# Up products of a gated block in eleven instead of twelve block products, with the stages beside them re-placed

## The chip, the cores and the metric

The kernel runs on one core of a Trainium2 chip. The metric is device time in microseconds (us), the median of several executions. The span in a profile is a little shorter than that time (628.2 us against 629.93 in the profiled run of the changed kernel). The first four executions of the kernel before span 0.25%, those of the changed kernel 0.7%. All executions that are compared here were of the fast state.

## The reference, cut to what matters

```python
# attention, for each of 4 batches and 8 heads, 768 tokens, head dimension 48
f = 1 / (1 + exp(-f_logit))
for t in range(S):
    state = f[t, :, None] * state + outer(k[t], v[t])
    y[t] = q[t] @ state
# x: the outputs as (3072 tokens, 384 channels)
a = x @ w_a            # 384 -> 1536
b = x @ w_b            # 384 -> 1536
out = (a * b) @ w_out  # 1536 -> 384
```

All of it is float32. The two products with `w_a` and `w_b` are called the up products here, the one with `w_out` the down product.

## The kernel before

Tokens come in eight blocks of 384, two per batch. A block needs two attention units, so there are 16 units. Each unit has stages on several engines: ScalarE's sigmoids, VectorE's scans, and small products on TensorE. A queue puts these stages between the large products.

The up product of one of the 12 output tiles takes three channel tiles for each of the two factors, 384 tokens at a time. ScalarE copies b out of PSUM, and VectorE multiplies it with a:

```python
def up(blk, ft):
    x, ps = xT[blk], {}
    for nm, w in (("b", w_b), ("a", w_a)):
        ps[nm] = ps_f.tile([128, 512], ...)[:, 0:BLK]
        for kt in range(NKT):                       # 3 channel tiles
            nc.tensor.matmul(ps[nm], lhsT=w[:, kt, ft * 128:ft * 128 + 128], rhs=x[:, kt],
                             start=kt == 0, stop=kt == NKT - 1)
    factors.append((blk, ft, ps))

def product():
    blk, ft, ps = factors.pop(0)
    b_sb = sb2.tile([128, BLK], ...)
    nc.scalar.copy(b_sb, ps["b"])
    # ...
    nc.vector.tensor_tensor(products[blk, part][:, :, i], a, b, ALU.mult)
```

The down product already works on pairs of token groups in seven instead of eight block products of 192 columns, with VectorE forming the sums (`s1` to `s4`) and the results. The kernel keeps TensorE's results in tiles of one memory, PSUM (a tile of 128x512 is called a bank here), and its operands in another, SBUF. Four PSUM banks serve up and down products together.

A unit's stages (the code is cut), and when they come (in steps; one output tile is a step, a down product is 3.5):

```python
def slot(u):                       # six calls, each up to the next yield
    within(u - 1); scores(u)       # TensorE; VectorE's mask
    yield
    next(nxt); yield               # unit u + 1: sigmoids (ScalarE)
    turn(u); across(u - 1); yield  # TensorE; ScalarE's copies
    next(nxt); yield               # scans of f (VectorE)
    gains(u); yield                # TensorE; VectorE's states
    next(nxt); next(nxt); yield    # scans of 1/f, products of q and k (VectorE)
# ...
at, when = m * a_batch + (-13.4, -0.8, 4.9, 13)[i], (0, 1, 2.2, 2.8, 3.4, 3.9)
```

## Time and profile before

| | before |
|---|---|
| time, median of 4 runs | 649.7 us |
| TensorE busy | 95% of 647.9 us |
| weight loads busy | 68% |
| VectorE, ScalarE busy | 45%, 29% |
| one instruction of 384 columns, undisturbed (46.64 us of the chain / 144) | 323.9 ns |
| one instruction of 192 columns, undisturbed (27.31 us / 168) | 162.6 ns |

A float32 product is two matmul instructions (1152 of L451 for 576 products). TensorE has no gap after 75 us (busy for 566.9 of the 566.9 us to the last product's end). This is the timeline of two halves of a tile in the last block (start, length, engine, line, operation, shapes; in brackets the idle time before and what ended it):

```profile
569.63 1.80 PEld L451 LDWEIGHTS f<-xT,w_a 128*128 128x128 f32 x6
569.95 2.10 PE L451 MATMUL f<-xT,w_a 128*128 128x384 f32 x6
570.20 0.48 ACT L466 COPY b_sb<-f 128x384 f32<-128x384 f32 x1 [5.89 <-PE f L451]
571.56 1.80 PEld L451 LDWEIGHTS f<-xT,w_b 128*128 128x128 f32 x6
571.88 2.10 PE L451 MATMUL f<-xT,w_b 128*128 128x384 f32 x6
572.15 0.56 DVE L471 TENSOR_TENSOR ab<-f,b_sb 128x384 f32<-128x384 f32 x1 [3.78 <-PE f L451]
573.50 1.80 PEld L451 LDWEIGHTS f<-xT,w_a 128*128 128x128 f32 x6
573.82 2.10 PE L451 MATMUL f<-xT,w_a 128*128 128x384 f32 x6
```

From start to start, the 12 instructions between 569.95 and 573.82 take 322.5 ns each. That is 1.4 ns less than the table has, because a piece's length also takes in its two ends (46.64 us less 144 x 322.5 ns leaves 0.2 us).

The lines show how loose this stretch is. ScalarE and VectorE each wait microseconds for TensorE, and TensorE writes a bank again only a whole tile later.

### The profile page before, as it was taken

Reading aid. Unit: us, or ns where it says so; the run is one execution under the profiler, and the core shown is the slowest. Engines: PE = TensorE matmul, PEld = TensorE weight load, DVE = VectorE, ACT = ScalarE, POOL = GpSimd, SP = SyncE. Lnnn points to the kernel's source line nnn. Section 1 sums busy time; section 2 is a strip of 40 time slices with the busy share of each in tenths; the row PEclk is TensorE's granted clock in tenths of the full one; section 3 lists DMA queues with packets and bytes.
Section 4 is the critical chain, followed back from the end, with each engine's and each line's share of the span. In section 5 each row is a group of like instructions: output and inputs, shape, how many; then the busy total and the mean of one; then the engine's idle time right before and its main releaser. Section 6 shows DMA issues by size and latency. Waiting matters only on the chain.

```text
span 647.9 us, 12250 instructions
## 1 busy us (share of the span) xinstructions
PE 614.6 (95%) x5202; PEld 442.0 (68%) x5202; DVE 289.7 (45%) x572; ACT 187.0 (29%) x328; POOL 65.6 (10%) x58
## 2 busy tenths in 40 slices
PE   0859899999999999999999999999999999999996
PEld 0626555559997566856698666966689655965696
DVE  6778345587774427161642345352444021311241
ACT  6577599632221322211201222122200212011100
POOL 6243154320010000000000000000000000000000
PEclk9969999999999999999999999999999999999999
DMA  9885874000332303130400124040001000000000
GB/s 223 232 266 157 193 260 147 1 2 2 97 92 72 92 1 92 38 80 1 93 24 26 47 46 92 14 105 1 19 1 37 14 19 19 1 26 0 1 24 30
DMA packets 30336, 43.56 MB, mean 67 GB/s; under 512 B 3776, under 2 KB 24896, under 8 KB 30272
## 3 DMA queue, kind: packets, MB, share of 16 engines
q1 hardware_dynamic: 29984, 42.38, 24.0%
q8 instruction: 43, 0.70, 0.4%
q10 hardware_dynamic: 288, 0.30, 0.2%
q14 instruction: 21, 0.17, 0.1%
HBM read 33.23 MB, written 4.72 MB: 59 GB/s over the span
## 4 chain that ended last, share of the span: by engine, by line
PE 92%; DMA 4%; ACT 1%; SPq 1%; DVE 0%; ACTq 0%; issue 0%; DVEq 0%
PE f L451 58%; PE f L508 26%; DMA xT<-y 2%; PE ps_y L409 2%; PE ps_y L388 2%; PE ps_x L354 2%; PE ps_x L308 2%; PE ps_x L335 1%; DMA q_in<-in_q_dram 1%; DMA raw<-in_moe_w_a_dram 1%; SPq L145 0%; PE f L335 0%; ACTq L436 0%; DVE y L422 0%; ACT bit L204 0%
## 5 line engine op out<-in xcount | busy, mean ns | idle before, releaser
L451 PE MATMUL f<-xT,w_b 128*128 128x384 f32 x576 | 206.9, 495 | 7.3 <-DVE w_b L211 5.6
L451 PE MATMUL f<-xT,w_a 128*128 128x384 f32 x576 | 203.4, 490 | 0.0
L451 PEld LDWEIGHTS f<-xT,w_a 128*128 128x128 f32 x576 | 110.2, 192 | 77.6 <-issue 2.3
L451 PEld LDWEIGHTS f<-xT,w_b 128*128 128x128 f32 x576 | 107.0, 191 | 78.6 <-DVE w_b L211 6.7
L471 DVE TENSOR_TENSOR ab<-f,b_sb 128x384 f32<-128x384 f32 x96 | 53.0, 555 | 199.1 <-PE f L451 147.9
L466 ACT COPY b_sb<-f 128x384 f32<-128x384 f32 x96 | 45.6, 476 | 228.9 <-PE f L451 219.6
L508 PE MATMUL f<-raw,h 128*128 128x192 f32 x432 | 73.7, 328 | 0.0
L508 PEld LDWEIGHTS f<-raw,h 128*128 128x128 f32 x432 | 70.2, 190 | 0.5
L261 POOL TENSOR_SCALAR inv<-inv 128x768 f32<-128x768 f32 x16 | 18.0, 1123 | 333.1 <-ACT inv L257 333.0
L508 PE MATMUL f<-w_out,ab 128*128 128x192 f32 x288 | 51.0, 327 | 0.0
L508 PEld LDWEIGHTS f<-w_out,ab 128*128 128x128 f32 x288 | 47.5, 190 | 1.8
L200 POOL TENSOR_SCALAR h<-h 128x768 f32<-128x768 f32 (+1 forms) x20 | 40.7, 2035 | 51.4 <-ACT h L197 49.7
L503 DVE TENSOR_TENSOR o<-f,u 128x192 f32<-128x192 f32 x36 | 12.9, 357 | 57.3 <-PE f L508 57.1
L308 PE MATMUL ps_x<-q_in,k_in 48*64 48x64 f32 x672 | 13.6, 226 | 15.6 <-DVE start L271 15.6
L276 DVE TENSOR_TENSOR_SCAN inv<-inv,start,zero 128x128 f32<-128x128 f32 x64 | 27.5, 471 | 0.0
L324 DVE TENSOR_TENSOR at<-ps_x,causal 128x768 f32<-128x768 f32 x14 | 13.4, 955 | 29.0 <-PE ps_x L308 29.0
L508 PE MATMUL f<-raw,ab 128*128 128x192 f32 x144 | 25.7, 328 | 0.0
L508 PE MATMUL f<-w_out,h 128*128 128x192 f32 x144 | 25.4, 326 | 0.0
L266 DVE TENSOR_TENSOR_SCAN f_in<-f_in,zero 128x384 f32<-128x384 f32 x28 | 25.2, 940 | 0.0
L370 DVE TENSOR_TENSOR st<-st,ps_x 128x96 f32<-128x96 f32 x80 | 20.2, 253 | 10.5 <-PE ps_x L354 8.0
L339 ACT COPY kT<-ps_x 128x768 f32<-128x768 f32 x12 | 9.6, 800 | 51.3 <-PE ps_x L335 51.3
L422 ACT COPY y<-ps_y 48x384 f32<-48x384 f32 (+1 forms) x43 | 20.5, 476 | 13.0 <-PE ps_y L409 8.4
(91 smaller groups left out, 456.6 us busy)
## 6 DMA issues: line engine op xcount, KB each, us to landing
q_in<-in_q_dram SPq DMA_DIRECT2D x32, 144.0 KB, 4.4
k_in<-in_k_dram SPq DMA_DIRECT2D x32, 144.0 KB, 3.7
v_in<-in_v_dram SPq DMA_DIRECT2D x16, 288.0 KB, 4.9
raw<-in_moe_w_out_dram SPq DMA_DIRECT2D x6, 768.0 KB, 4.2
out_dram<-o SPq DMA_DIRECT2D x24, 192.0 KB, 1.9
f_in<-in_f_logit_dram SPq DMA_DIRECT2D x28, 144.0 KB, 3.1
xT<-y SPq DMA_DIRECT2D x46, 72.0 KB, 2.2
raw<-in_moe_w_b_dram SPq DMA_DIRECT2D x4, 768.0 KB, 7.3
```

The lines of the kernel that those rows point to most:

```text
L200: nc.gpsimd.tensor_scalar(h, h, HI_MAX, None, ALU.min)
L261: nc.gpsimd.tensor_scalar(inv, inv, EXP_K, 1.0, ALU.mult, ALU.add)
L266: nc.vector.tensor_tensor_scan(F[:, c], F[:, c], none, math.exp(MIDDLE), ALU.mult, ALU.add)
L276: nc.vector.tensor_tensor_scan(inv[:, w], inv[:, w], none[:, 0:C], first, ALU.mult, ALU.add)
L308: nc.tensor.matmul(ps[h][SUB * p:SUB * p + SUB, o:o + SUB], lhsT=kf[r, tokens(n, c, p)], rhs=qf[r, tokens(n, c, p)], start=True, stop=True,)
L324: nc.vector.tensor_tensor(to, x, tri.broadcast_to((128, *lead, 2 * NC, SUB)), ALU.mult)
L370: nc.vector.tensor_tensor(st[:, j], before, new, ALU.add)
L422: copy(y[r:r + rows, :, p], ps[p][e:e + rows, 0:BLK].rearrange("r (o m) -> r o m", m=SUB))
L451: nc.tensor.matmul(ps[nm], lhsT=w[:, kt, ft * 128:ft * 128 + 128], rhs=x[:, kt], start=kt == 0, stop=kt == NKT - 1,)
L466: nc.scalar.copy(b_sb, ps["b"])
L471: nc.vector.tensor_tensor(products[blk, part][:, :, i], a, b, ALU.mult)
L508: nc.tensor.matmul(to, lhsT=x[:, i], rhs=w[:, i], start=first and i == 0, stop=i == HFT - 1, skip_group_check=True)
```

## The change

From block 2 on, two output tiles, two channel tiles and two token halves make a 2x2 by 2x2 product, done in seven block products by sums; the third channel tile is added in four. That is eleven products of 192 columns per factor in place of twelve. The additions go to VectorE, the intermediate results through ScalarE into SBUF. The units' stages are cut and placed anew. Storage is shared to make room: one tile `groups` for the products and the pair's scratch, one for `spare` combinations, and a single `inv` scratch for the later units.

```diff
+    def up_pair(blk, j):
+        # ... blocks a11..a22 of the weights, b11..b22 of the tokens, a1, a2, b1, b2 the third channel tile
+        order = (0, 1, 2, 3) if next(turns) else (2, 3, 0, 1)
+        x0, x1, m0, m1 = (ps_f[i][:, 0:2 * HT].rearrange("p (g t) -> p g t", g=2) for i in order)
+        # times(): for both factors g, one product = two instructions of 192 columns each
+        times(x0, a11, b11, True)
+        nc.scalar.copy(p1, x0)
+        times(x1, a12, b21, True)
+        times(m1, s1, t1, True)
+        nc.scalar.copy(p5, m1)
+        times(x0, s2, t2)
+        nc.scalar.copy(u2, x0)
+        times(m0, a22, t4, True)
+        times(m0, a2, b1)
+        times(x0, s3, t3)
+        nc.scalar.copy(u3, x0)
+        add(1, 0, m0, u3)
+        yield
+        times(m1, s4, b22)
+        times(m1, a1, b2)
+        add(0, 1, m1, u2)
+        times(x1, a1, b1)
+        add(0, 0, x1, p1)
+        times(x0, a2, b2)
+        add(1, 1, x0, p5)
+        # ... two multiplications a * b
+        yield
# ...
     def slot(u):
+        next(nxt, None)              # sigmoids
+        yield
         if u > 2 * NQ: within(u - 1)
         if u < NU: scores(u)
-        yield
         next(nxt, None)              # scans of f
         yield
         # turn(u), across(u - 1)
         yield
-        next(nxt, None)
-        yield
         # gains(u)
         yield
         next(nxt, None)              # scans of 1/f
+        yield
         next(nxt, None)              # products of q and k
         yield
# ... when the stages come, in steps of half a pair, by the unit's place in its batch
+                (2.6, 3.6, 4.6, 5.6, 7.6, 9.6),
+                (10.6, 12.3, 13.3, 14.3, 17.1, 19.1),
+                (20.1, 21.1, 22.1, 23.1, 25.1, 27.8),
+                (28.8, 29.8, 30.3, 31.3, 33.3, 36.1),
```

(The remarks in the code are mine.) The first `yield` of a pair is its middle, the second its end.

More of the change, by code (lines that the diff above doesn't have):

```diff
@@ L1 @@
+import itertools
 import math
@@ L65 @@
     ident = fixed([128, 128], "ident")
-    w_a = fixed([128, NKT, DFF], "w_a")
-    w_b = fixed([128, NKT, DFF], "w_b")
+    w_ba = fixed([128, 2, NKT, DFF], "w_ba")
     w_out = fixed([128, NFT, DM], "w_out")
     bad = fixed([1, 1], "bad", I32)
-    weights = (w_a, w_b, w_out)
+    weights = (w_ba, w_out)
     with ExitStack() as pools:
@@ L81, in by_quotients @@
     B, H, D, S = q.shape
-    w_a, w_b, w_out = weights
-    NKT, NFT, DM = w_a.shape[1], w_out.shape[1], out.shape[1]
+    w_ba, w_out = weights
+    w_b, w_a = (w_ba[:, i] for i in range(2))
+    NKT, NFT, DM = w_ba.shape[2], w_out.shape[1], out.shape[1]
     NH = S // BLK
@@ L98, in by_quotients @@
     sb3 = ctx.enter_context(tc.tile_pool(name="sb3", bufs=3))
-    ab_pool = ctx.enter_context(tc.tile_pool(name="ab", bufs=4))
     raw_pool = ctx.enter_context(tc.tile_pool(name="raw", bufs=4))
     ps_a = ctx.enter_context(tc.tile_pool(name="ps_a", bufs=1, space=bass.MemoryType.PSUM))
-    ps_f = ctx.enter_context(tc.tile_pool(name="ps_f", bufs=4, space=bass.MemoryType.PSUM))
     def fixed(shape, name):
@@ L119, in by_quotients @@
     whole = fixed([128, 1], "whole")
-    sign = fixedp.tile([128, PIECE], BF16, tag="sign", name="sign")
-    bits = [fixedp.tile([128, PIECE], U32, tag=f"bit{i}", name=f"bit{i}") for i in range(3)]
+    groups = fixed([128, 2 * NTG, NFT * 128], "groups")
+    spare = fixed([128, 3 * HFT * (DM // 2)], "spare")
+    bits = [spare[:, PIECE * i:PIECE * i + PIECE].bitcast(U32) for i in range(3)]
+    sign = spare[:, 3 * PIECE:3 * PIECE + PIECE // 2].bitcast(BF16)
+    invs = [fixed([128, 2 * BLK], "inv"), spare[:, 3 * PIECE + PIECE // 2:3 * PIECE + PIECE // 2 + 2 * BLK]]
     tails = fixed([128, NU], "tails")
@@ L178, in load_weights @@
                 if len(raws) in EARLY:
-                    raw = ab_pool.tile([128, NTG * HFT * 128 // 2], mybir.dt.uint64, tag="ab", name="ab")
+                    raw = groups[:, EARLY.index(len(raws))].bitcast(mybir.dt.uint64)
                 else:
@@ L241, in by_quotients @@
     live = {}
-    firsts = ab_pool.tile([128, NQ, 2, BLK], FP32, tag="ab", name="ab")
+    firsts = groups[:, len(EARLY)].rearrange("p (u n s) -> p u n s", u=NQ, n=2)
     products_of_f = {u: firsts[:, u] if u in FIRST else sets[u % NSET]["f"] for u in range(NU)}
@@ L253, in front @@
         F = halves(products_of_f[u])
-        inv = sb2.tile([128, 2 * BLK], FP32, tag="inv", name="inv")
+        inv = invs[u % 2 if u < 2 * NQ else 0]
         if u in FIRST:
@@ L285, in by_quotients @@
     y_banks = [ps_y[:, p] for p in range(2)]
+    ps_f = [ps_a.tile([128, 512], FP32, tag=f"ps_f{i}", name=f"ps_f{i}") for i in range(4)]
+    idle = list(range(4))
+    turns = itertools.cycle((0, 1))
     def tokens(n, c, p):
@@ L296, in pair, with give_back @@
     def pair(spare=False):
-        return [ps_f.tile([128, 512], FP32, tag="f", name="f") if spare else ps_x[:, i] for i in range(2)]
+        return [ps_f[idle.pop(0)] if spare else ps_x[:, i] for i in range(2)]
+    def give_back(ps):
+        idle.extend(i for x in ps for i, bank in enumerate(ps_f) if bank is x)
     def scores(u, spare=False):
@@ L325, in scores @@
         live[u]["at"] = at
+        give_back(ps)
     def turn(u, spare=False):
@@ L340, in turn @@
         live[u]["kT"] = kT
+        give_back(ps)
     def gains(u):
@@ L422, in across @@
             copy(y[r:r + rows, :, p], ps[p][e:e + rows, 0:BLK].rearrange("r (o m) -> r o m", m=SUB))
+        give_back(ps)
         y = y.rearrange("r (n c) p m -> r n (c p m)", n=2)
@@ L440, in across, with products @@
             load_unit(u + NSET)
-    products = {}
+    def products(blk):
+        first = (NTG, 0)[blk] if blk < 2 else blk % 2
+        return groups[:, first:first + NTG].rearrange("p g (k t) -> p g k t", k=NFT)
     factors = []
@@ L448, in up @@
         for nm, w in (("b", w_b), ("a", w_a)):
-            ps[nm] = ps_f.tile([128, 512], FP32, tag="f", name="f")[:, 0:BLK]
+            ps[nm] = ps_f[idle.pop(0)]
             for kt in range(NKT):
                 nc.tensor.matmul(
-                    ps[nm],
+                    ps[nm][:, 0:BLK],
                     lhsT=w[:, kt, ft * 128:ft * 128 + 128],
@@ L465, in product @@
         b_sb = sb2.tile([128, BLK], FP32, tag="b_sb", name="b_sb")
-        nc.scalar.copy(b_sb, ps["b"])
-        part, i = divmod(ft, HFT)
-        if i == 0:
-            products[blk, part] = ab_pool.tile([128, NTG, HFT, 128], FP32, tag="ab", name="ab")
-        a, b = (x.rearrange("p (g t) -> p g t", g=NTG) for x in (ps["a"], b_sb))
-        nc.vector.tensor_tensor(products[blk, part][:, :, i], a, b, ALU.mult)
+        nc.scalar.copy(b_sb, ps["b"][:, 0:BLK])
+        a, b = (x.rearrange("p (g t) -> p g t", g=NTG) for x in (ps["a"][:, 0:BLK], b_sb))
@@ new lines, in product, with by_pairs, combine_w_ba @@
+        nc.vector.tensor_tensor(products(blk)[:, :, ft], a, b, ALU.mult)
+        give_back(ps.values())
+    HT = BLK // 2
+    sums_of_w, sums_of_x = [], {}
+    def by_pairs(k):
+        w = w_ba[:, :, k].rearrange("p g (j two c) -> p g two j c", two=2, c=128)
+        return w[:, :, 0], w[:, :, 1]
+    def combine_w_ba():
+        (a11, a21), (a12, a22) = by_pairs(0), by_pairs(1)
+        for _ in range(4):
+            raw = raw_pool.tile([128, PIECE], mybir.dt.uint64, tag="raw", name="raw")
+            sums_of_w.append(raw.bitcast(FP32).rearrange("p (g j c) -> p g j c", g=2, c=128))
+        s1, s2, s3, s4 = sums_of_w
+        for to, x, y, op in (
+            (s3, a11, a21, ALU.subtract),
+            (s1, a21, a22, ALU.add),
+            (s2, s1, a11, ALU.subtract),
+            (s4, a12, s2, ALU.subtract),
+        ):
+            for g in range(2):
+                nc.vector.tensor_tensor(to[:, g], x[:, g], y[:, g], op)
+            yield
@@ new lines, in blocks_of_x, with combine_x @@
+    def blocks_of_x(blk, k):
+        return (xT[blk][:, k, HT * i:HT * i + HT] for i in range(2))
+    def combine_x(blk):
+        (b11, b12), (b21, b22) = blocks_of_x(blk, 0), blocks_of_x(blk, 1)
+        tiles = (sb2.tile([128, BLK], FP32, tag="b_sb", name="b_sb") for _ in range(2))
+        t1, t2, t3, t4 = sums_of_x[blk] = [t[:, HT * i:HT * i + HT] for t in tiles for i in range(2)]
+        for to, x, y in ((t1, b12, b11), (t2, b22, t1), (t3, b22, b12), (t4, b21, t2)):
+            nc.vector.tensor_tensor(to, x, y, ALU.subtract)
@@ new lines, in up_pair, with times, add @@
+    def up_pair(blk, j):
+        (a11, a21), (a12, a22), (a1, a2) = (by_pairs(k) for k in range(NKT))
+        (b11, b12), (b21, b22), (b1, b2) = (blocks_of_x(blk, k) for k in range(NKT))
+        s1, s2, s3, s4 = sums_of_w
+        t1, t2, t3, t4 = sums_of_x[blk]
+        order = (0, 1, 2, 3) if next(turns) else (2, 3, 0, 1)
+        x0, x1, m0, m1 = (ps_f[i][:, 0:2 * HT].rearrange("p (g t) -> p g t", g=2) for i in order)
+        p1, p5, u2, u3 = groups[:, 2 * NTG - 1].rearrange("p (i g t) -> i p g t", i=4, g=2)
+        c = groups[:, 2 * NTG - 2].rearrange("p (g k i t) -> p g k i t", g=2, k=2, i=2)
+        def times(to, w, x, start=False):
+            for g in range(2):
+                nc.tensor.matmul(
+                    to[:, g], lhsT=w[:, g, j], rhs=x, start=start and g == 0, stop=True, skip_group_check=True
+                )
+        def add(k, i, x, y):
+            nc.vector.tensor_tensor(c[:, :, k, i], x, y, ALU.add)
+        times(x0, a11, b11, True)
[18 more added lines that the diff above has]
+        add(1, 1, x0, p5)
+        b, a = (c[:, g].rearrange("p k i t -> p k (i t)").rearrange("p k (g t) -> p g k t", g=NTG) for g in range(2))
+        to = products(blk)
+        for k in range(2):
+            nc.vector.tensor_tensor(to[:, :, 2 * j + k], a[:, :, k], b[:, :, k], ALU.mult)
+        yield
@@ L482, in combine_w_out @@
         )
-        for _ in range(4):
-            raw = raw_pool.tile([128, PIECE], mybir.dt.uint64, tag="raw", name="raw")
-            combos.append(raw.bitcast(FP32)[:, 0:HFT * HM].rearrange("p (k m) -> p k m", k=HFT))
-        t1, t2, t3, t4 = combos
-        nc.vector.tensor_tensor(t3, b22, b12, ALU.subtract)
+        combos.extend(spare.rearrange("p (i k m) -> i p k m", i=3, k=HFT))
+        t1, t2, t4 = combos
+        combos.insert(2, b12)
         nc.vector.tensor_tensor(t1, b12, b11, ALU.subtract)
@@ L490, in combine_w_out @@
         nc.vector.tensor_tensor(t4, b21, t2, ALU.subtract)
+        nc.vector.tensor_tensor(b12, b12, b22, ALU.subtract)
     def down(pair):
-        (blk0, g0), (blk1, g1) = pair
         b11, b21, b22 = (w_out[:, HFT * i:HFT * i + HFT, HM * j:HM * j + HM] for i, j in ((0, 0), (1, 0), (1, 1)))
         t1, t2, t3, t4 = combos
-        a11, a21 = products[blk0, 0][:, g0], products[blk1, 0][:, g1]
+        (blk0, g0), (blk1, g1) = pair
+        a11, a12 = (products(blk0)[:, g0, HFT * i:HFT * i + HFT] for i in range(2))
+        a21, a22 = (products(blk1)[:, g1, HFT * i:HFT * i + HFT] for i in range(2))
         def block():
@@ L510, in times @@
                 )
-        s3 = add(block(), a11, a21, ALU.subtract)
+        s3 = add(block(), a21, a11, ALU.subtract)
         yield
-        x, m = (ps_f.tile([128, 512], FP32, tag="f", name="f") for _ in range(2))
+        x, m = ps_f[0:2] if next(turns) else ps_f[2:4]
         x0, x1, m0, m1 = (t[:, HM * i:HM * i + HM] for t in (x, m) for i in range(2))
@@ L519, in down @@
         product()
-        a12, a22 = products[blk0, 1][:, g0], products[blk1, 1][:, g1]
         s1 = add(block(), a21, a22)
@@ L571, in slot @@
         next(nxt, None)
+        yield
         next(nxt, None)
@@ L710, in by_quotients @@
             if b:
-                rest += [(up, 2 * b, ft) for ft in range(NFT)] + [(down, b, tuple(even[0:2]))]
-                rest += [(up, 2 * b + 1, ft) for ft in range(NFT)]
-            else:
-                rest += [(down, b, tuple(even[0:2]))]
-            rest += [(down, b, (even[2], odd[0])), (down, b, tuple(odd[1:]))]
+                rest += [(up_pair, 2 * b, j) for j in range(NFT // 2)] + [(down, b, tuple(even[1:]))]
+                rest += [(up_pair, 2 * b + 1, j) for j in range(NFT // 2)]
+            else:
+                rest += [(down, b, tuple(even[1:]))]
+            rest += [(down, b, (even[0], odd[0])), (down, b, tuple(odd[1:]))]
         slots = {s: slot(s) for s in range(2 * NQ, NU + 1)}
@@ L719, in by_quotients @@
         queue = [(2 * NFT - 4 + d, fronts[2 * NQ]) for d in (0, 0.9, 1.8, 1.8)]
-        for s in slots:
-            m, i = divmod(s - 2, 2 * NQ)
-            at, when = m * a_batch + (-13.4, -0.8, 4.9, 13)[i], (0, 1, 2.2, 2.8, 3.4, 3.9)
-            if s < 3 * NQ + 1:
-                at = 2 * NFT
-                when = ((-1.1, -1.1, 0.5, 0.5, 1, 2.5), (3.4, 3.4, 4, 4, 4.5, 6), (7, 7, 7.5, 7.5, 8, 9.5))[s - 2 * NQ]
-            queue += [(at + d, slots[s]) for d in when]
+        begun_early = (
+            (22.9, 22.9, 24.5, 25, 26.3, 26.3),
+            (27.3, 27.3, 27.8, 28.3, 29.8, 29.8),
+            (30.3, 30.3, 31.3, 31.3, 32.3, 33.3),
+            (33.4, 33.4, 33.9, 33.9, 36.1, 38.1),
+            (39.1, 40.1, 41.1, 41.1, 42.1, 44.1),
+        )
+        for s in slots:
+            m, i = divmod(s, 2 * NQ)
+            when = (
+                (2.6, 3.6, 4.6, 5.6, 7.6, 9.6),
+                (10.6, 12.3, 13.3, 14.3, 17.1, 19.1),
+                (20.1, 21.1, 22.1, 23.1, 25.1, 27.8),
+                (28.8, 29.8, 30.3, 31.3, 33.3, 36.1),
+            )[i]
+            queue += [((m - 1) * a_batch + d, slots[s]) for d in when] if s > 4 * NQ else [
+                (d, slots[s]) for d in begun_early[s - 2 * NQ]
+            ]
+        sums = combine_w_ba()
+        queue += [(d, sums) for d in (15.6, 16.6, 17.6, 18.6)]
         queue.sort(reverse=True, key=lambda x: x[0])
@@ L749, in by_quotients @@
                 continue
-            if (blk, i) == (B - 1, tuple(even[0:2])):
+            if what is up_pair:
+                for _ in up_pair(blk, i):
+                    step += 1
+                    beside()
+                if i == 2 + blk % 2:
+                    ahead = down(rest[n + NFT // 2 - i][2])
+                    next(ahead)
+                continue
+            if (blk, i) == (B - 1, tuple(even[1:])):
                 sum_held()
@@ L760, in by_quotients @@
                     next(ahead)
+                if part == 4 and rest[n + 1:] and rest[n + 1][0] is up_pair:
+                    combine_x(rest[n + 1][1])
                 step += 0.5
@@ L764, in by_quotients @@
             next(this, None)
-            if (blk, i) == (B - 1, tuple(even[0:2])):
+            if (blk, i) == (B - 1, tuple(even[1:])):
                 check_held()
@@ L781, in by_levels @@
     HP = H // 2
-    w_a, w_b, w_out = weights
-    NKT, NFT, DM = w_a.shape[1], w_out.shape[1], out.shape[1]
+    w_ba, w_out = weights
+    w_b, w_a = (w_ba[:, i] for i in range(2))
+    NKT, NFT, DM = w_ba.shape[2], w_out.shape[1], out.shape[1]
     NB = S // BLK
@@ L1043, in ffn @@
                 for ft in range(NFT):
-                    nc.tensor.matmul(
-                        o,
-                        lhsT=ab[ft][:, tg * 128:tg * 128 + 128],
-                        rhs=w_out[:, ft],
-                        start=ft == 0,
-                        stop=ft == NFT - 1,
-                    )
+                    y = ab[ft][:, tg * 128:tg * 128 + 128]
+                    nc.tensor.matmul(o, lhsT=y, rhs=w_out[:, ft], start=ft == 0, stop=ft == NFT - 1)
+                    if ft < NFT // 2:
+                        nc.tensor.matmul(
+                            o[:, DM // 2:], lhsT=y, rhs=w_out[:, ft + NFT // 2, DM // 2:], start=False, stop=False
+                        )
                 o_sb = sb2.tile([128, DM], FP32, tag="o_sb", name="o_sb")
```

## The prediction

> **What bounds the kernel now.** I read the page first, then the stretches (busy time of each engine between two times), then the chain of waits in order of time, then single groups by shape, then the timeline of one stretch. The busy shares:
>
> ```profile
> PE 614.6 (95%) x5202; PEld 442.0 (68%) x5202; DVE 289.7 (45%) x572; ACT 187.0 (29%) x328; POOL 65.6 (10%) x58
> PE   0859899999999999999999999999999999999996
> PE 92%; DMA 4%; ACT 1%; SPq 1%; DVE 0%; ACTq 0%; issue 0%; DVEq 0%
> ```
>
> TensorE is busy 95% of the span, all its idle time lies in the first five of 40 slices, and the chain that ended last is 92% TensorE. From 75 us on there is no gap. [...] Two pieces of the chain have no attention work in them:
>
> ```profile
> 567.98 46.64 PE f L451 x144
> 614.62 27.31 PE f L508 x168
> ```
>
> L451 is the product with w_a and w_b, L508 the down product. 46.64 us / 144 = 323.9 ns for one instruction of 384 columns; 27.31 us / 168 = 162.6 ns for one of 192. A float32 product is two instructions (1152 for 8 blocks x 12 tiles x 2 factors x 3 channel tiles = 576 products). The stretches, columns being us, length, then busy time per engine:
>
> ```profile
> 201.20:323.15 121.95, 121.95 (x1038) 80.32 (x1037) 51.07 (x111) 28.45 (x55) 3.34 (x4) 1.00 0.22 55
> 323.15:474.15 151.00, 151.00 (x1303) 109.08 (x1302) 62.33 (x129) 30.36 (x61) 3.34 (x4) 1.00 0.16 40
> ```
>
> The second stretch is one period: three down products, two blocks of 12 tiles, four attention units. At the two rates, 288 instructions of 384 columns are 93.3 us and 3 x 84 of 192 are 41.0 us, together 134.3; the other 16.7 us are four units at 4.2 us. Nothing is left for waits: the period is TensorE work throughout, at granted clock 1.00. So TensorE time removed there is removed from the end, one for one, unless something new makes TensorE wait.
>
> [...] The trace has 162.6 and 323.9, so halving the columns costs next to nothing per instruction: 2 x 162.6 = 325.2 against 323.9.
> [...]
>
> **The change part by part.**
> (1) The products of blocks 2 to 7, six of eight. The two output tiles of a pair, two of the three channel tiles and two token halves form a 2x2 by 2x2 product done in seven instead of eight; the third channel tile takes four as before. Per pair of tiles, before: 2 tiles x 2 factors x 3 products x 2 = 24 instructions x 323.9 = 7.77 us. After: 11 x 2 factors x 2 = 44 instructions x 162.6 = 7.15 us. Saved 0.62 us; with 6 blocks x 6 pairs = 36 pairs, 22.3 us. This lies wholly on the path.
>
> (2) Its additions, which lie beside TensorE. These rows show their costs before:
>
> ```profile
> L471 DVE TENSOR_TENSOR ab<-f,b_sb 128x384 f32<-128x384 f32 x96 | 53.0, 555 | 199.1 <-PE f L451 147.9 <-ACT b_sb L466 51.2
> L503 DVE TENSOR_TENSOR h<-ab,h 128x768 f32<-128x768 f32 x12 | 11.5, 958 | 14.1 <-PE f L508 14.1
> L466 ACT COPY b_sb<-f 128x384 f32<-128x384 f32 x96 | 45.6, 476 | 228.9 <-PE f L451 219.6 <-DVE ab L471 8.1
> ```
>
> Per pair VectorE goes from 2 multiplications to 4 additions and 2 multiplications of 384: 6 x 0.555 = 3.3 us instead of 1.1; ScalarE from 2 copies to 4: 1.9 us instead of 0.95. Against 7.15 us of TensorE there is room. Over 36 pairs: +80 us of VectorE, +34 us of ScalarE. Per block four differences of the tokens of 192 columns (4 x 0.357 = 1.4 us, 8.6 in all); once, eight differences of weights of 768 (8 x 0.958 = 7.7 us). VectorE should come to about 386 us, ScalarE to about 221.
>
> (3) Waits inside a pair, the point where this can fail. Four banks x0, x1, m0, m1; a group of four instructions is 0.65 us. x0 is written, copied out, and accumulated on again after two groups (1.30 us), then once more after two groups. In the timeline of the last down product a copy begins 0.2 us after the next group has begun (614.45 + 1.95 = 616.40, copy at 616.60). A copy of 0.476 is done at about 0.7 us, so 0.6 us of slack. The next pair takes the other order of banks: its first group lands in m0, read long before; its third in x1, last read by an addition that ends about 0.7 us after the pair's last group has begun, against 0.65 + 1.30 us until the write. No stall by itself.
>
> (4) The stages of the attention units. Read against the new generator, VectorE's long stages (scans of 2 x 0.94 and 6 x 0.47 us, mask 0.96) fall at ends of pairs or in down products; in the middle of a pair fall only ScalarE's sigmoids and the transposes with their copies. At the end of a pair VectorE has about 1.8 us of the pair left plus up to 3 us of stage, and its next addition is due 5.3 us into the next pair. ScalarE's 2 us in the middle end before the next copy is due, about 3 us later. So I expect hardly a stall from these. TensorE's own work for a unit is unchanged.
>
> (5) Once: the weight sums fall between about 118 and 132 us, where VectorE also converts w_out and multiplies, and run into the sums of w_out (5.9 us from 128.6 to 134.5 before). About 2 us of backlog is added behind that; the up product has a spare pair of banks, so I put 0 to 2 us there. In the three down products at 147 to 201 us VectorE is at 41.9 of 53.9 us already, and the units' scratch is single instead of double: another 0 to 2 us.
>
> (6) The down products keep their count (signs and pairs only). One in-place difference replaces a copy, same duration. The start before 75 us is only renamed storage: no change.
>
> Sum: 649.75 - 22.3 + about 1.5 (between 0 and 5) = 628.9 us.
>
> **Rivals.**
> *VectorE or ScalarE becomes the bound inside a pair.* For it: they go from 0.5 to about 0.6 of VectorE, [...] and TensorE now waits for copies inside a product (each 0.6 us slack), not only between products. A ScalarE copy delayed behind three copies of y (1.4 us) would cost 0.5 to 1 us. Against: the stages' placement avoids it, and the down product, built alike, runs at 162.6 ns with its waits. If every pair lost 0.3 us: +11 us, 638.
> *Loading weights binds.* The loads double for the same columns, and the last down products show loading busy 27.02 of 27.30 us, against 27.54 of 46.62 for the 384 columns. If a load were longer than its matmul, 44 of them would cost more. Against: those down products sustain exactly the 192-column matmul rate with a load each. At 170 ns the 36 pairs would give back 36 x 44 x 7.4 ns = 12 us, 640.
> *False dependencies of shared storage.* Scratch, products and combinations now live in slices of one tile. If a copy into scratch had to wait for the pair's multiplications before it (done 1.8 us into the next pair), x0 would be late by about 0.4 us per pair: +14 us. Against: the slices are contiguous and disjoint from those that TensorE reads in a down product.
> *The gain is hidden anyway by transfers.* DMA share after 200 us is at most 0.35 in 20 us and no wait for a transfer shows there; I dismiss it.
>
> **Range and chances.** No stalls at all gives 627.4; a few tenths better is possible if the new placement trims losses at the joints of attention and products (the 4.2 us per unit). Up to 5 us of stalls gives 632.5. So 625.5 to 633 should hold it 8 times in 10. The 2% mark is 636.8: it takes over 9 us of stalls, as in the rivals, to miss it. Faster 0.92, within 2% 0.07, slower 0.01.
>
> **What would show it.** TensorE instructions 5202 + 36 x 20 = 5922; the chain still above 90% TensorE. The period of two blocks with three down products falls from 151.0 to about 143.6 us, the last block without attention from 46.6 to about 42.9. Undisturbed pairs at 162.6 ns per instruction confirm step 1; 165 or more points to the loads. Idle TensorE with releaser ScalarE or VectorE within the new products after 200 us would confirm the first or third rival, and the prediction would be wrong if it exceeds 5 us. VectorE about 386 us and ScalarE about 221 us check step 2; a gap between 125 and 201 us checks step 5.

## The result, and the profile after

The changed kernel takes 630.07 us (628.46 to 632.8, four runs) against 649.7. The ratio is 0.9705, with a 95% interval from 0.9669 to 0.9742. A ratio here is the mean time of one kernel's fast runs over that of the other's fast runs of the same rounds, so it is not quite the ratio of the medians. In a later call, with five rounds, the same kernel had 630.47 us and 0.9712.

The page after: the engines' busy time, the slices of TensorE and of its weight loads, the chain that ended last, and the rows of the new additions and multiplications:

```profile
PE 592.5 (94%) x5922; PEld 535.6 (85%) x5922; DVE 378.2 (60%) x748; ACT 221.3 (35%) x400; POOL 63.0 (10%) x58
PE   0859899999999999999999999999999999999995
PEld 0626555558998999999999999999999999999995
PE 88%; DMA 4%; DVE 2%; ACT 2%; SPq 2%; issue 1%; ACTq 0%; DVEq 0%
L547 DVE TENSOR_TENSOR groups<-ps_f,groups 128x384 f32<-128x384 f32 x144 | 80.1, 557 | 118.5 <-ACT groups L559 99.3
L572 DVE TENSOR_TENSOR groups<-groups 128x384 f32<-128x384 f32 x72 | 36.6, 550 | 0.0
```

TensorE still carries the span, with 720 more instructions in 22 us less busy time. Loading weights rose from 68% to 85%, VectorE from 45% to 60%. The pieces of the chain without attention work, and the two periods (the stretches that were 151.0 us each):

```profile
551.51 43.10 PE ps_f L542 x264
594.60 27.32 PE ps_f L610 x168
...
204.00:348.44 144.44, 144.09 (x1542) 140.57 (x1541) 92.28 (x192) 41.88 (x85) 3.33 (x4) 1.00 0.24 59
348.44:492.36 143.92, 143.92 (x1543) 140.54 (x1542) 85.71 (x175) 40.01 (x82) 2.50 (x3) 1.00 0.14 36
```

43.10 / 264 = 163.3 ns for an instruction of 192 columns in the new products, where 46.64 us / 144 gave 323.9 for one of 384 before. (From start to start it is 162.5: see the pair below.) I laid the two chains side by side, from the start of one block to that of another:

| stretch | before | after | difference |
|---|---|---|---|
| start to the end of the first 24 tiles | 147.4 | 146.7 | -0.7 |
| to block 2 (three down products) | 53.8 | 57.3 | +3.5 |
| block 2 to block 4 | 151.0 | 144.4 | -6.6 |
| block 4 to block 6 | 151.0 | 143.9 | -7.1 |
| block 6 to the last product | 138.7 | 129.6 | -9.2 |

Of the +3.5 in the second row, 2.4 us is only moved: three products of a unit that came after the start of block 2 now come before it (199.44 to 201.82 us in the trace after). The last row gains them back. So 1.1 us of the row is lost, and the last row saves 6.8. At 12 pairs per row, each of the three last rows should save 7.4 us at the prediction's 0.62 us per pair, and 7.1 at the 0.59 that the starts of the instructions give (worked out below).

The timeline of a pair in the last block shows how tight the new products are:

```profile
561.29 0.81 PE L542 MATMUL ps_f<-b_sb,w_ba 128*128 128x192 f32 x4
561.55 0.48 ACT L555 COPY groups<-ps_f 128x384 f32<-128x384 f32 x1 [0.18 <-PE ps_f L542]
561.78 0.68 PEld L542 LDWEIGHTS ps_f<-xT,w_ba 128*128 128x128 f32 x4
561.94 0.81 PE L542 MATMUL ps_f<-xT,w_ba 128*128 128x192 f32 x4
562.43 0.68 PEld L542 LDWEIGHTS ps_f<-b_sb,raw 128*128 128x128 f32 x4
562.59 0.81 PE L542 MATMUL ps_f<-b_sb,raw 128*128 128x192 f32 x4
...
568.44 0.81 PE L542 MATMUL ps_f<-b_sb,w_ba 128*128 128x192 f32 x4
```

The copy (L555) reads x0 and ends at 562.03. The products that write x0 again load their weights from 562.43. The next pair comes to the same place at 568.44, 7.15 us after 561.29: 44 instructions of 162.5 ns.

### The profile page after: what moved, and what is told of

The parts are those of the page before. It is cut to its first block, busy times and chain, and to the rows that moved or that the text cites. A ratio compares the mean times of both kernels' runs of the same rounds, so it can differ in the third digit from the quotient of the medians.

```text
span 628.2 us, 13968 instructions
## 1 busy us (share of the span) xinstructions
PE 592.5 (94%) x5922; PEld 535.6 (85%) x5922; DVE 378.2 (60%) x748; ACT 221.3 (35%) x400; POOL 63.0 (10%) x58
## 4 chain that ended last, share of the span: by engine, by line
PE 88%; DMA 4%; DVE 2%; ACT 2%; SPq 2%; issue 1%; ACTq 0%; DVEq 0%
PE ps_f L542 41%; PE ps_f L610 23%; PE ps_f L469 14%; DMA xT<-y 2%; PE ps_y L401 2%; PE ps_y L422 2%; PE ps_x L319 2%; PE ps_x L367 2%; PE ps_x L347 1%; SPq L154 1%; DMA raw<-in_moe_w_b_dram 1%; SPq L450 1%; DMA out_dram<-o 1%; ACT y L435 1%; DVE h L605 0%
## 5 line engine op out<-in xcount | busy, mean ns | idle before, releaser
L542 PE MATMUL ps_f<-xT,w_ba 128*128 128x192 f32 x864 | 155.4, 327 | 0.0
L547 DVE TENSOR_TENSOR groups<-ps_f,groups 128x384 f32<-128x384 f32 x144 | 80.1, 557 | 118.5 <-ACT groups L559 99.3
L542 PEld LDWEIGHTS ps_f<-xT,w_ba 128*128 128x128 f32 x864 | 142.3, 190 | 0.5
L469 PE MATMUL ps_f<-xT,w_ba 128*128 128x384 f32 x288 | 98.4, 502 | 7.9 <-DVE w_ba L216 5.9
L469 PEld LDWEIGHTS ps_f<-xT,w_ba 128*128 128x128 f32 x288 | 55.3, 195 | 47.8 <-DVE w_ba L216 7.0
L542 PE MATMUL ps_f<-b_sb,raw 128*128 128x192 f32 x432 | 82.0, 326 | 0.0
L542 PEld LDWEIGHTS ps_f<-b_sb,raw 128*128 128x128 f32 x432 | 72.2, 190 | 0.0
L610 PE MATMUL ps_f<-w_out,h 128*128 128x192 f32 x288 | 52.0, 330 | 0.3 <-DVE o L605 0.3
L610 PE MATMUL ps_f<-w_out,groups 128*128 128x192 f32 x288 | 50.9, 327 | 0.0
L610 PE MATMUL ps_f<-spare,h 128*128 128x192 f32 x288 | 49.6, 328 | 0.2 <-DVE h L605 0.2
L610 PEld LDWEIGHTS ps_f<-w_out,groups 128*128 128x128 f32 x288 | 47.3, 190 | 0.1
```

The lines of the kernel that those rows point to most:

```text
L469: nc.tensor.matmul(ps[nm][:, 0:BLK], lhsT=w[:, kt, ft * 128:ft * 128 + 128], rhs=x[:, kt], start=kt == 0, stop=kt == NKT - 1,)
L542: nc.tensor.matmul(to[:, g], lhsT=w[:, g, j], rhs=x, start=start and g == 0, stop=True, skip_group_check=True)
L547: nc.vector.tensor_tensor(c[:, :, k, i], x, y, ALU.add)
L610: nc.tensor.matmul(to, lhsT=x[:, i], rhs=w[:, i], start=first and i == 0, stop=i == HFT - 1, skip_group_check=True)
```

## The experiments

Every kernel gave a correct result. Each edit is against the changed kernel unless it says otherwise.

**1. The old products in the new frame (twelve_whole).**

```diff
-                rest += [(up_pair, 2 * b, j) for j in range(NFT // 2)] + [(down, b, tuple(even[1:]))]
-                rest += [(up_pair, 2 * b + 1, j) for j in range(NFT // 2)]
+                rest += [(up, 2 * b, ft) for ft in range(NFT)] + [(down, b, tuple(even[1:]))]
+                rest += [(up, 2 * b + 1, ft) for ft in range(NFT)]
```

> The changed kernel with its new placement, storage and weight sums, but with blocks 2 to 7 in twelve whole products of 384 columns as before (in the last unit alone the stage after the mask comes two steps later, for order's sake). Theory (the gain is TensorE time of fewer columns, the re-placement is about neutral): 650.5 us, between 649 and 652, TensorE instructions back at 5202. Rival (the re-placement of the stages carries part of the gain): clearly below 648.

Measured: 652.19 us (651.74 to 652.54), ratio 1.0037 (1.0023 to 1.0051). The new frame alone does not help the old products; it costs about 3 us, a little more than expected. (TensorE's waits there name VectorE's outputs of the down product with 1.5 us; the rest I did not trace.) Set against the changed kernel at 630.07, 36 pairs save 22.1 us, or 0.61 us each; 0.62 was worked out. The two numbers come from different calls; the ratios to the kernel before, 1.0037 and 0.9705, give 21.6 us and 0.60.

**2. The old products in halves (twelve_halves).** Each product of blocks 2 to 7 in the kernel of experiment 1 is cut into two of 192 columns:

```diff
-                    rhs=x[:, kt],
-                    start=kt == 0,
+                    rhs=x[:, kt, cols],          # for each half of the tokens
+                    start=kt == i == 0,
```

> As the run with twelve whole products, but each product of blocks 2 to 7 in two halves of 192 columns: 48 instructions per pair of tiles, twice the loads, no new additions. Theory (an instruction of 192 columns costs 162.6 ns with its load hidden): 48 x 162.6 = 7.80 us per pair against 7.77, so +1.1 us over the run with whole products, about 651.6. Rival (weight loads bind at this size): several us more, at 170 ns an instruction +14 us.

Measured: 654.1 us (653.29 to 654.47), ratio 1.0067, so 1.9 us more than experiment 1. The piece of its chain for the last block:

```profile
571.50 47.00 PE ps_f L472 x288
```

47.00 / 288 = 163.2 ns over the piece, and 162.5 from start to start. Cutting and doubling the loads is nearly free, and it brings nothing by itself. Against this kernel the changed one has the same kind of instruction, and 264 in place of 288 of them: 43.10 / 47.00 = 0.917, which is 11/12.

**3. Eleven products from block 4 on only (from_fifth).**

```diff
-                rest += [(up_pair, 2 * b, j) for j in range(NFT // 2)] ...
+                rest += [(up_pair, 2 * b, j) for j in range(NFT // 2)] if b > 1 else [(up, 2 * b, ft) ...]
```

(and the same for the odd block)

> Eleven products only in blocks 4 to 7, blocks 2 and 3 whole as before. Theory (0.62 us per pair, 36 pairs): 12 pairs give back 7.4 us, so 637.5 us. If the gain lay elsewhere than in the pairs, the time would stay near 630 or go all the way back.

Measured: 636.53 us (636.09 to 637.44), ratio 0.9802 (0.9786 to 0.9819). Twelve pairs fewer cost 6.5 us, 0.54 us each; from here back to none, 24 pairs cost 15.7 us, 0.65 each. The gain scales with the pairs.

**4. The new products with the old stages (old_stages).** `slot` and the queue's times are those of the kernel before, the products are the new ones.

> The changed kernel with the attention units' stages cut and placed as in the kernel before. Theory (VectorE's long scans in the middle of a pair hold up its additions and with them TensorE's banks): about 637 us, 633 to 642, with idle TensorE in the new products released by VectorE. Rival (VectorE at 60% has room anywhere, placement is neutral): 629 to 631.

Measured: 649.27 us (646.79 to 650.98, 12 runs), ratio 0.9997 (0.9985 to 1.0009). I had expected 637. The whole gain is gone. VectorE's busy time is 374.0 us against 378.2, so its amount of work is not the cause. This is its timeline around one stall:

```profile
242.89 0.56 DVE L547 TENSOR_TENSOR groups<-ps_f,groups 128x384 f32<-128x384 f32 x1 [3.61 <-ACT groups L559]
...
245.81 0.83 DVE L281 TENSOR_TENSOR_SCAN inv<-inv,start,zero 128x128 f32<-128x128 f32 x2
...
248.48 0.95 DVE L284 TENSOR_TENSOR k_in<-k_in,inv 128x768 f32<-128x768 f32 x1
249.35 1.48 DVE L547 TENSOR_TENSOR groups<-ps_f,groups 128x384 f32<-128x384 f32 x3
...
249.95 0.92 PE L542 MATMUL ps_f<-xT,w_ba 128*128 128x192 f32 x4 [3.53 <-DVE groups L547]
```

The first addition of the pair runs at 242.89. Then come a unit's states, scans and products, 6 us of them, put there in the middle of the pair. Only at 249.35 do the other three additions follow, and TensorE has waited for the bank for 3.5 us. In this trace TensorE shows 11.4 us of such waits in six places. Part of the rest is in matmuls that the trace shows stretched rather than idle: after the wait above, four instructions took 1.49 us instead of 0.81. There the granted clock, the share of its full clock that TensorE was allowed, had fallen. The view of busy times has it third from the end:

```profile
251.30:254.60 3.30, 3.30 (x12) 3.30 (x11) 0.46 (x1) 0.96 (x2) 0.00 (x0) 0.50 0.00 0
```

It is 0.50 for 3.4 us (251.2 to 254.7), and again for 3.4 us (404.8 to 408.3) after the other wait of the same length. Each time costs about 1.7 us, an estimate: half of the 3.4. In the changed kernel it is 1.00 from 47 to 620 us. So 11.4 us of waits and 3.4 us of clock have a place; the remaining 4 us I did not break down. Period from block 2 to block 4: 355.94 - 202.27 = 153.7 us, against 144.4.

**5. Old stages, but never in the middle of a pair (old_at_ends).** Against experiment 4:

```diff
-                for _ in up_pair(blk, i):
+                for half, _ in enumerate(up_pair(blk, i)):
                     step += 1
-                    beside()
+                    if half:
+                        beside()
```

> The run with the old stages, but stages due in the middle of a pair wait for its end; nothing else differs. Theory (what cost 19 us there is VectorE's long work between a pair's first and last additions): most of it comes back, 632 to 640, the remainder where two of the old stages now fall together behind one pair. Rival (the old stages cost because inputs arrive late or because the units come at other times): still above 643.

Measured: 641.34 us (640.4 to 642.51), ratio 0.9886. About 8 of the 19 us come back, less than I expected; the number lies between what the two theories gave. The trace shows what is left at its largest place:

```profile
277.71 1.80 DVE L271 TENSOR_TENSOR_SCAN f_in<-f_in,zero 128x384 f32<-128x384 f32 x2
...
284.73 0.95 DVE L284 TENSOR_TENSOR k_in<-k_in,inv 128x768 f32<-128x768 f32 x1
285.60 1.95 DVE L547 TENSOR_TENSOR groups<-ps_f,groups 128x384 f32<-128x384 f32 x4
...
286.20 2.35 PE L542 MATMUL ps_f<-xT,w_ba 128*128 128x192 f32 x8 [1.91 <-DVE groups L547]
```

Four of the old stages now fall together behind one pair: VectorE is busy with them from 277.7 to 285.6, 7.9 us, and all four additions of the next pair come after. The pair before began at 276.88, so two pairs at 7.15 us would end at 291.2; in the chain the second one ends at 295.3, so 4 us are lost there: 1.9 us in the wait, and about 1.7 because the granted clock is 0.50 from 286.8 to 290.3. (The other wait of 1.9 us, before 437.1, was not followed by a lower clock.) TensorE's waits for VectorE in the new and the down products come to 6.2 us in four such places. So the middle of a pair is shown to be part of the cause, and lumps of stages behind one pair another. I did not follow the whole of the 11 us.

**6. One order of the banks (one_order).**

```diff
-        order = (0, 1, 2, 3) if next(turns) else (2, 3, 0, 1)
+        order = (0, 1, 2, 3) if next(turns) else (0, 1, 2, 3)
```

> The changed kernel with the four banks in the same order in every pair. The next pair's first group then writes the bank that the pair's last addition reads, which ends about 0.8 us after the pair's last group. Theory (the alternating order hides this): about 0.8 us per joint of two pairs without attention work between, some 20 to 30 joints, so 646 to 656 us. Rival (TensorE has slack there anyhow): 630.

Measured: 654.57 us (654.11 to 654.77), ratio 1.0078, 24.5 us more than the changed kernel. TensorE's waits:

```profile
PE ps_f L542 <- DVE groups L547: 14.6, 22, 0.9
```

22 joints wait up to 0.9 us for the pair's last addition, and three down products do so too (1.9 us). In the last block the pairs follow at 8.06 us (579.86 to 587.92) instead of 7.15. At 0.91 us each, these 25 places make 22.8 of the 24.5 us. Without the alternation the change would have lost all its gain.

**7. One copy made twice, then three times (copy_twice, copy_thrice).**

```diff
-        nc.scalar.copy(u2, x0)
+        for _ in range(2):               # or 3
+            nc.scalar.copy(u2, x0)
```

> ScalarE's second copy of a pair (the one between two accumulations on x0) is made twice, with the same result. Theory (0.6 us of slack behind it, the copy takes 0.48): within 2 us of the changed kernel, so 630 to 632. If ScalarE were already late, +0.48 us per pair: 647.

> The same copy three times. Theory (0.96 us more against 0.6 us of slack): 0.35 us per pair, 36 pairs, +12.6 us, so 640 to 646, with TensorE waiting for ScalarE. Rival (ScalarE at 35% of the span has room, average shares decide): 630 to 632.

Measured: 633.11 us (632.65 to 633.69) and 651.97 us (650.84 to 653.0), ratios 0.975 and 1.0042. That is 0.08 and 0.61 us per pair, both above what I had expected. The slack is smaller than 0.6 us. With three copies:

```profile
580.67 1.50 ACT L556 COPY groups<-ps_f 128x384 f32<-128x384 f32 x3 [0.23 <-PE ps_f L542]
580.90 0.68 PEld L542 LDWEIGHTS ps_f<-xT,w_ba 128*128 128x128 f32 x4
581.06 0.81 PE L542 MATMUL ps_f<-xT,w_ba 128*128 128x192 f32 x4
582.22 0.62 PEld L542 LDWEIGHTS ps_f<-b_sb,raw 128*128 128x128 f32 x4 [0.64 <-ACT groups L556]
582.22 0.92 PE L542 MATMUL ps_f<-b_sb,raw 128*128 128x192 f32 x4 [0.34 <-ACT groups L556]
```

The copies end at 582.17. Load and matmul both start at 582.22, where the load otherwise starts 0.16 us ahead of its matmul (562.43 and 562.59 above). So the wait holds the load too, and the real slack is 562.43 - 562.03 - 0.05 = 0.35 us. A second copy (0.5 us) overruns it by 0.15, of which 0.08 shows. ScalarE was at 39% of the span in the slow kernel.

**8. VectorE's multiplications four times (dve_three_more).**

```diff
-        for k in range(2):
+        for k in (0, 1) * 4:
             nc.vector.tensor_tensor(to[:, :, 2 * j + k], a[:, :, k], b[:, :, k], ALU.mult)
```

> The two multiplications at the end of a pair are made four times in place of once, with the same result: +3.3 us of VectorE per pair, 119 us in all, its share from 60% to about 77%. Theory (what counts is when the next addition is due, 5.3 us into the next pair plus about 1.2 us of slack in the banks): free in a pair without a long stage (1.8 + 3.3 = 5.1 us), late by 1 to 2 us behind the scans and masks, some 12 to 18 places: +10 to +25 us, 640 to 655. Rival (VectorE below 80% never matters): 630 to 632.

Measured: 652.35 us (651.53 to 653.95), ratio 1.0054, 22.3 us more. VectorE was busy for 73% of the span. Where there are no stages, the extra 3.3 us per pair are free, as expected: the last block has

```profile
568.88 43.11 PE ps_f L542 x264
```

against 43.10. But the largest waits are not where I had put them. They are in the down product that follows a block (14.5 us in 6 places for VectorE's sums there), which stand behind the multiplications in VectorE's queue; in the new products only 1.0 us shows. After two of these waits (3.0 us before 557.1, 2.6 before 618.5) the granted clock is 0.50 for 3.4 us again, some 3.4 us of loss in all (60 instructions from 557.09 take 11.67 us, where 60 from 153.05 take 9.95); after two more of 3.0 us (before 326.5 and 477.3) it is not. So 18.9 of the 22.3 us have a place.

**9. Two trims of the changed kernel (again, later7, later7_pool).**

```diff
-            (33.4, 33.4, 33.9, 33.9, 36.1, 38.1),
+            (33.4, 33.9, 34.4, 34.4, 36.1, 38.1),
# later7_pool also:
-        nc.sync.dma_start(out=out[r0:r0 + 128], in_=o[:, 0])
+        nc.gpsimd.dma_start(out=out[r0:r0 + 128], in_=o[:, 0])   # and the other output
```

> The changed kernel once more, on the chip of this call, for comparison: 630, ratio 0.970 to before.

> One unit's stages in the last down product of the first batch come half a down step later, so that its scores no longer stand before VectorE's product of k (TensorE came to them at 195.5 us and began at 196.4). Theory: 0.5 to 1 us less than the changed kernel run beside it, seen in the stretch before block 2; in the time itself within the noise, 629 to 630.

> As the last, and the down products' outputs are sent from GpSimd's queue rather than behind nine issues of one unit on SyncE's. Theory (VectorE waited 2.8 us for such an output at 344 us, TensorE 0.3 us): another 0.3 to 1 us, 628.5 to 630. Rival (sends from GpSimd are slower or disturb VectorE): 631 or more.

Measured, five rounds each: 630.47 (ratio 0.9712, 0.9693 to 0.9731), 629.07 (0.9699, 0.9682 to 0.9716) and 629.86 us (0.9703, 0.9682 to 0.9725). In later7 the wait aimed at (0.7 us of TensorE for the product of k) is gone from the trace. From the end of the first 24 tiles to block 2 takes 56.4 us instead of 57.3. But from there to the last product it takes 0.7 us more than in the run again, so 0.2 us is left. The outputs sent from GpSimd's queue removed VectorE's 2.8 us wait for them without a measurable gain. The intervals overlap: no version that clearly beats the changed kernel was found.

## Why the prediction was right

The four kernels that stages and products make (the two of the lower left and upper right have the changed kernel's storage and weight sums too):

| | old stages | new stages |
|---|---|---|
| twelve products | 649.3 (before) | 652.2 |
| eleven products | 649.3 | 630.1 |

**The main term, right, but put about 1 us too high.** Step 1 put 0.62 us on a pair and 22.3 us on the whole. Experiments 1 and 3 measured 0.60 to 0.61 us for 36 pairs and 0.54 to 0.65 for parts of them. Experiment 2 shows that what is saved is one product in twelve: same instructions, 11/12 of the number. The sum divided the length of a piece by its instructions, and so spread the piece's ends over them (323.9 ns). From start to start the traces have 322.5 and 162.5 ns. With these, a pair saves 24 x 322.5 - 44 x 162.5 ns = 0.59 us, and 36 pairs 21.2 us. Experiment 2 fits the same numbers: 48 x 162.5 - 24 x 322.5 ns is 0.06 us per pair, 2.2 us in all, where 1.1 was expected and 1.9 measured.

**What lies beside TensorE, right.** ScalarE came to 221.3 us (221 said) and VectorE to 378.2 (386 said). The new additions took 557 ns and the multiplications 550, where 555 was taken; 768 and 192 elements, taken as 958 and 357, took that in the trace before. The last block went from 46.6 to 43.1 us (42.9 said), the period to 144.4 and 143.9 (143.6 said). At 0.59 us per pair they would be 43.1 and 143.9.

**The stalls, of the right size.** The sum had about 1.5 us, between 0 and 5. The span fell by 19.7 us. Against the 22.3 that were worked out 2.6 us are missing; against 21.2, only 1.5 us net were lost. About 1.1 of this is in the three down products before block 2, where step 5 had put up to 2: TensorE waited for VectorE's product of k. The other half of step 5, up to 2 us of stall behind the weight sums at 118 to 132 us, did not appear: the run of up products from 74 us on took TensorE 72.58 us, against 72.64 before.

**The order of the stages, right in kind and far too lightly weighed.** Step 4 read from the queue that the new stages hardly stall, and the trace agrees. What the prediction did not see is how much hangs on it. It spoke of rivals that cost 11 to 14 us. With the old stages the time is 649.3, 19 us more. Nor did it see that after a wait of 1.9 to 3.5 us TensorE's granted clock was 0.50 for about 3.4 us in five places (experiments 4, 5 and 8; after three such waits it was not), which adds to what the wait itself costs. The rival "VectorE or ScalarE becomes the bound" is real, and it was the placement that kept it away. The average load does not tell the two apart: VectorE was at 58% in the kernel that lost everything.

**The slack behind a copy, wrong in size.** Step 3 had 0.6 us. It is 0.35 us, because the weight load waits as well and it starts 0.16 us before its matmul; the hand-over of 0.05 us comes on top. At one copy this did not matter.

**The banks, right.** Step 3 saw the alternation as what keeps the joint of two pairs free; experiment 6 puts 24.5 us on it.

**Loads as a rival, out.** Loading weights rose to 85% busy, and at 86% (experiment 2) the rate was still 162.5 ns from start to start. In the last block of the changed kernel matmuls and loads are both busy for the whole 43.1 us. False dependencies of the shared storage were not tested by a run of their own, but a loss of 0.4 us per pair is not in the trace: undisturbed pairs follow at 7.15 us, which 44 instructions of 162.5 ns fill.

**One sign that failed.** I had said the chain would stay above 90% TensorE. It shows 88%. In three places (from 189, 331 and 537 us, together 24 us) the chain now passes through VectorE, or through ScalarE and the transfers. TensorE's gaps at their ends are only 0.7, 0.3 and 0.2 us. So the sign failed without a loss to match.

## What to carry to other kernels

Fewer products on a saturated TensorE were worth their instructions here (0.60 us measured per pair, 0.59 worked out), but additions moved to another engine put that engine's queue between two products, and then the order of its work decides (19 us here). Place that engine's long work where the next result is due late, look for the first reader of each bank, and measure the placement together with the products: here each of the two alone gave nothing. When a copy stands between two accumulations, count its slack to the weight load, not to the matmul (0.35 us here, where 0.6 was reckoned). To find the time of one instruction, take it from start to start, not from the length of a piece.
